# Forward attention of a fused block on Trainium2: the order of a step's score matmuls, P V and filler matmuls on TensorE

## The chip, the core and the metric

The kernel runs on one core of one Trainium2 chip. The metric is the device time in microseconds of one execution of the whole program. Each time of a kernel is a median of several executions; the profile is one further execution, recorded by the hardware profiler.

## What is computed

The program computes a transformer block with attention and a gated feed-forward part side by side, and the gradients of its six inputs, all in one launch. Cut to what matters:

```python
xn = layernorm(x)                                   # x: 1 x 2048 x 448
q, k, v = split(xn @ wqkv)                          # 16 heads of 28
p  = softmax(q @ k^T * 28**-0.5)                    # 16 x 2048 x 2048
o  = p @ v
y  = x + concat(o) @ wo + (silu(xn @ w_gate) * (xn @ w_up)) @ w_down   # F = 1792
out_0 = y;  out_1 .. out_6 = gradients for grad_out of x, wqkv, wo, w_gate, w_up, w_down
```

## The kernel before, in words

The instructions of every engine are issued in the order in which the Python code names them (`manual_schedule`, L59); each engine works its own list from front to back. Waits between engines are set by the tile framework, from the tiles that instructions read and write and from the buffers that a pool has to give.

The program has four stages: a prologue (layer norm, projections of head group 0), the forward loop (L588 to L621), the backward loop of attention (L830 to L915) with the remaining products of the feed-forward part between its matmuls, and a tail for the gradient of x.

The forward loop has 256 steps `(g, qc, kt)`: 4 groups of 4 heads, 4 chunks of 512 queries, 16 tiles of 128 keys. In one step:

- **Scores, two halves.** A head has 28 columns, padded to 32, so that the four heads of a group stand on the partitions 0, 32, 64 and 96 of `qT` and `kT`. One matmul (L600) with a contraction of 32 rows gives the transposed scores of one head, 128 keys x 512 queries. A *half* is two such matmuls, on two row tiles of TensorE: half 0 on rows 0 and 32, half 1 on rows 64 and 96. They fill one `s_ps` tile of two PSUM banks. The pool `ps_s` has two such buffers (L108), so half 0 of a step takes the buffer of half 0 of the step before, and half 1 that of half 1.
- **Exponentials.** Behind each half ScalarE runs one `Exp` over 128 x 1024 (L604) from `s_ps` into an `eT` tile in SBUF (seven buffers, L107).
- **P V.** `pv(i)` (L575 to L586) multiplies the four `eT` pieces of step i with the values of the four heads: four matmuls (L582) on four column tiles, summed over 16 steps in `o_ps`, a pool with one buffer (L109). In step i the call is `pv(i - 2)`, and it stands between the two halves (L606, L607). At the last key tile `pv` calls `o_items` (L467), which issues a ScalarE copy of `o_ps` (L470) and pushes four transposes and sixteen small matmuls, with their DMAs, to the front of the filler queue.
- **Fillers.** `fill(pace)` (L617) then takes other TensorE work from a queue: the three products of the feed-forward part (L383), its weight gradients (L357), the projections of the next head group (L180), the pushed items of `o_items`. Each has a fixed cost (`MM`, `MMD`), and `pace` (L594) is the cost that is left divided by the steps that are left. Fillers write to `ps_f` (three buffers). The last matmul of a gate product issues a `Tanh` on ScalarE (L393), and VectorE does the rest.

So TensorE's list for a step reads: half 0, P V of two steps ago, half 1, fillers. ScalarE's list reads: Exp 0, (copy of `o_ps` once in 16 steps), Exp 1, (Tanh once in some steps).

In the text, S0 and S1 are the two halves, E0 and E1 their exponentials, and F is the time from the first filler to the S0 of the next step.

Of the kernel before, what the change touches and what calls it, by code (L numbers as in the profile page):

```python
# [12 lines left out]
FP32 = mybir.dt.float32  # L13
# [11 lines left out]
P = 128  # L25
# [12 lines left out]
def kernel(  # L38
# [69 lines left out]
    ps_s = bst.enter_context(tc.tile_pool(name="ps_s", bufs=2, space=PSUM))  # L108
# [99 lines left out]
    def sp_layouts(g):  # L208
        for tq, dst in ((0, spq_d), (1, spk_d)):
            s_ = stg.tile([P, NT, P], BF16, name="sp_stage")  # L210
            sp.dma_start_transpose(out=s_[:], in_=qk_tiles[(g, tq)][:])
            pool.dma_start(out=dst[g], in_=s_[:].rearrange("p t c -> p (t c)"))
# [96 lines left out]
    def fill(budget):  # L309

        while budget > 0.05:
            if not cur:
                if not queue:
                    return
                cur.extend(queue.popleft())
            cost, fn = cur.popleft()
            fn()
            budget -= cost
            left[0] -= cost

    def push(jobs, front=False, behind=0):
        left[0] += sum(c for job in jobs for c, _ in job)
        if front:
            first = [queue.popleft() for _ in range(min(behind, len(queue)))]
            queue.extendleft(reversed(first + jobs))
        else:
            queue.extend(jobs)

    def proj_items(g):
        out = []  # L330
        for tq in range(3):
            for sc in range(4):
                box = {}

                def go(c, tq=tq, sc=sc, box=box):
                    if c == 0:
                        box["m"] = proj_unit(g, tq, sc, "dve")
                    box["m"](c)
                out.append([(MM, lambda c=c, go=go: go(c)) for c in range(4)])
        out.append([(0.0, lambda: proj_done(g))])  # L340
        return out
# [204 lines left out]
    def load_pair(pr, parts):  # L546

        g, r = pr // 2, 64 * (pr % 2)
        q = qkp.tile([P, S], BF16, name="qT")
        k = qkp.tile([P, S], BF16, name="kT")  # L550
        qd[pr] = (q, k)
        n = S // parts
        return [lambda i=i, dst=dst, r0=r0, src=src: sp.dma_start(
                    out=dst[r0:r0 + 64, i:i + n], in_=src[g, r:r + 64, i:i + n])
                for r0, srcs in ((0, (qT_d, kT_d)), (64, (dOT_d, vT_d)))
                for dst, src in zip((q, k), srcs) for i in range(0, S, n)]

    def load_group(g, parts, kpool):

        spt[g] = [qkp.tile([P, NT, P], BF16, name="v_sp"), kpool.tile([P, S], BF16, name="vT"),  # L560
                  qkp.tile([P, NT, P], BF16, name="O_sp")]
        spt[g][1] = spt[g][1][:].rearrange("p (t c) -> p t c", c=P)
        n = NT // parts
        return [lambda i=i, t=t, src=src: sp.dma_start(
                    out=t[:, i:i + n, :].rearrange("p t c -> p (t c)"), in_=src[g, :, i * P:(i + n) * P])
                for t, src in zip(spt[g], (spq_d, spk_d, spo_d)) for i in range(0, NT, n)]
# [6 lines left out]
    pv_next = [0]  # L573

    def pv(i):  # L575
        g, qc, kt = steps[i]
        if kt == 0:
            o_cur["o"] = ps_o.tile([P, 512], FP32, name="o_ps")
        o_ps, v = o_cur["o"], v_tiles[g]
        e = eTs.pop(i)  # L580
        for hh in range(4):
            pe.matmul(o_ps[HP * hh:HP * (hh + 1), :], lhsT=v[:, kt, HP * hh:HP * (hh + 1)],  # L582
                      rhs=e[hh // 2][:, hh % 2, :], start=(kt == 0), stop=(kt == NT - 1),
                      tile_position=(0, HP * hh), skip_group_check=True)
        if kt == NT - 1:
            o_items(g, qc, o_ps)  # L586

    for i, (g, qc, kt) in enumerate(steps):  # L588
        if kt == 0 and qc == 1:
            push([[(0.0, lambda g=g: sp_layouts(g))]], front=True)  # L590
        if kt == 0 and qc == 2 and g + 1 < G:
            push(proj_items(g + 1), front=True)
        qT, kT = qk_tiles[(g, 0)], qk_tiles[(g, 1)]
        pace = left[0] / (nst - i)  # L594
        eTs[i] = []
        for half in range(2):
            s_ps = ps_s.tile([P, 2, 512], FP32, name="s_ps")
            for j in range(2):
                r = HP * (2 * half + j)
                pe.matmul(s_ps[:, j, :], lhsT=kT[r:r + HP, kt * P:(kt + 1) * P],  # L600
                          rhs=qT[r:r + HP, qc * 512:(qc + 1) * 512],
                          start=True, stop=True, tile_position=(r, 0))
            e = ep.tile([P, 2, 512], BF16, name="eT")
            act.activation(out=e[:], in_=s_ps[:], func=ACT.Exp, scale=SCALE)  # L604
            eTs[i].append(e)
            if half == 0 and i >= 2:  # L606
                pv(i - 2)  # L607
        if g == G - 1 and qc == 2:
            if kt == 0:
                first = load_pair(0, 1) + load_group(0, 1, vp)  # L610
            elif kt % 2 and first:
                first.pop(0)()
        if i in (6, 8, 10, 12):
            j = i // 2 - 3
            sp.dma_start_transpose(out=woT[:, :, j * P:(j + 1) * P], in_=wo_pad[:, j, :])
        pv_next[0] = max(0, i - 1)
        fill(pace)  # L617
    while pv_next[0] < nst:
        pv(pv_next[0])
# [210 lines left out]
    for k in range(N + 2 * UW):  # L830
        W, pos = k // UW, k % UW
        if k < N:
# [16 lines left out]
            s_ps = ps_sd.tile([P, 2, 512], FP32, name="sd")  # L849
# [162 lines left out]
```

## Time and profile before

| | |
|---|---|
| median of 3 runs | 1563.34 us (1561.85 to 1567.34) |
| the profiled execution | 1562.89 us, of which the profile's span is 1561.1 us |
| forward loop in the trace | S0 of the first step at 31.1 us, S1 of the last at 664.4 us |
| TensorE matmuls (PE) busy | 1447.1 us of the span |
| ScalarE (ACT) busy | 1190.1 us |
| VectorE (DVE) busy | 1098.9 us |

How to read it: PE stands for TensorE's matmuls and PEld for its weight loads. Matmuls are pipelined, so that two that follow each other overlap in the records; the distance from one start to the next is what a matmul costs its engine, not its recorded duration. A row of the timeline has the start, the time until the last of its instructions ended, the engine, the line, what is written from what, the shapes, and how many instructions it joins; in brackets stand the idle time of the engine ahead of it and what ended it. A row of a stretch has its length and, for each engine, busy time and number of instructions, then the granted TensorE clock, the share of the DMA engines in use and GB/s.

### The profile page before, as it was taken

The numbers are of one execution on the slowest core, as the hardware profiler recorded it, in microseconds if no ns is written. First come the engines' busy times: TensorE is split into PE (matmuls) and PEld (weight loads), VectorE is DVE, ScalarE is ACT, GpSimd is POOL, SyncE is SP. The second block draws the span as 40 slices with busy tenths as digits, with TensorE's granted clock in tenths as the row PEclk, the third lists the DMA queues.
The fourth block names the chain that finished last, engine by engine and source line by source line (L and its number), as shares of the span: only waits on it lengthen the run. The fifth ranks groups of instructions, "written<-read, shape, count | busy, mean of one in ns | idle before, by whom it ended". The sixth has DMA issues, their size and how long they took to land.

```text
span 1561.1 us, 32024 instructions
## 1 busy us (share of the span) xinstructions
PE 1447.1 (93%) x12176; PEld 606.3 (39%) x12176; DVE 1098.9 (70%) x1421; ACT 1190.1 (76%) x1333; POOL 396.1 (25%) x664
## 2 busy tenths in 40 slices
PE   6999999899999999988998988989999899999986
PEld 3233333333333333333333444434335333544353
DVE  7664655455655666467877887979888789888925
ACT  6899998688787877766776777878778778888823
POOL 4342333344434444411010111110102111111033
PEclk9999999899999999989999999999999999999998
DMA  9985756875967699879999999999999999999993
GB/s 231 190 162 120 145 116 137 164 146 127 198 131 155 134 186 212 170 164 222 204 214 200 192 202 217 198 197 200 207 208 199 196 194 196 185 188 213 184 281 123
DMA packets 682106, 285.12 MB, mean 183 GB/s; under 512 B 637136, under 2 KB 650464, under 8 KB 681952
## 3 DMA queue, kind: packets, MB, share of 16 engines
q1 hardware_dynamic: 652016, 210.03, 72.7%
q0 software_dynamic: 25968, 64.53, 17.1%
q10 hardware_dynamic: 3968, 8.52, 1.6%
q8 instruction: 95, 1.56, 0.4%
q14 instruction: 59, 0.48, 0.1%
HBM read 67.34 MB, written 63.44 MB: 84 GB/s over the span
## 4 chain that ended last, share of the span: by engine, by line
PE 63%; DMA 14%; ACT 9%; DVE 6%; issue 5%; SPq 1%; POOL 1%; DVEq 0%; POOLq 0%; ACTq 0%
PE s_ps L600 8%; PE f_ps L357 8%; DMA dsT<-ds 8%; PE f_ps L383 7%; PE sd L851 6%; ACT E L869 5%; PE acc L748 4%; PE aux L718 4%; PE o_ps L582 4%; PE aux L775 4%; PE aux L795 4%; DVE ds L880 3%; PE aux L712 3%; ACT dsT L782 3%; PE sd L862 3%
## 5 line engine op out<-in xcount | busy, mean ns | idle before, releaser
L880 DVE TENSOR_TENSOR ds<-sd,E 128x1024 bf16<-128x1024 f32 x512 | 611.2, 1220 | 131.8 <-DMA dsT<-ds 47.8
L869 ACT ACTIVATE E<-sd 128x1024 bf16<-128x1024 f32 x512 | 516.7, 1024 | 171.7 <-PE sd L862 133.6
L604 ACT ACTIVATE eT<-s_ps 128x1024 bf16<-128x1024 f32 x512 | 497.9, 1024 | 103.8 <-PE s_ps L600 102.9
L862 PE MATMUL sd<-kT,qT 32*128 32x512 bf16 x1024 | 203.2, 390 | 23.6 <-ACT E L869 22.7
L851 PE MATMUL sd<-kT,qT 32*128 32x512 bf16 x1024 | 201.9, 391 | 20.1 <-DVE ds L880 17.9
L748 PE MATMUL acc<-ds,v_sp 128*32 128x512 bf16 x1024 | 205.7, 397 | 0.7 <-DVE ds L880 0.7
L748 PE MATMUL acc<-E,O_sp 128*32 128x512 bf16 x1024 | 205.5, 397 | 0.2 <-ACT dkv_o L754 0.2
L600 PE MATMUL s_ps<-qT,kT 32*128 32x512 bf16 x1024 | 200.1, 388 | 1.5 <-ACT eT L604 1.1
L422 POOL DMA_DIRECT2D hd_d<-fT x168 | 126.8, 767 | 17.2 <-DVE fT L407 9.9
L383 PE MATMUL f_ps<-xnT,wgu 128*128 128x512 bf16 x448 | 120.2, 387 | 3.4 <-DVE w_sb L409 3.4
L763 POOL DMA_DIRECT2D dqkv_d<-dkv_o x64 | 39.3, 619 | 293.1 <-ACT dkv_o L754 290.9
L600 PEld LDWEIGHTS <-kT 32*128 32x128 bf16 x1024 | 48.7, 91 | 159.8 <-issue 158.1
L718 PE MATMUL aux<-W,ck 128*128 128x448 bf16 x448 | 107.1, 356 | 3.3
L851 PEld LDWEIGHTS <-qT 32*128 32x128 bf16 x1024 | 51.0, 91 | 149.2 <-issue 141.2
L582 PE MATMUL o_ps<-eT,v_sp 128*32 128x512 bf16 x1024 | 103.2, 394 | 0.0
L357 PE MATMUL f_ps<-xn_sp,f_sp 128*128 128x448 bf16 x448 | 99.1, 354 | 0.0
L748 PEld LDWEIGHTS <-O_sp 128*32 128x32 bf16 x1024 | 50.4, 93 | 113.5 <-issue 103.7
L775 PE MATMUL aux<-ident_bf,ds 128*128 128x128 bf16 x1024 | 81.6, 224 | 11.6 <-DVE dq_acc L807 5.7
L862 PEld LDWEIGHTS <-qT 32*128 32x128 bf16 x1024 | 65.0, 91 | 61.7 <-issue 57.8
L357 PEld LDWEIGHTS <-f_sp 128*128 128x128 bf16 x672 | 58.3, 98 | 73.8 <-issue 23.7
L775 PEld LDWEIGHTS <-ds 128*128 128x128 bf16 x1024 | 63.7, 100 | 40.9 <-issue 40.2
L395 DVE SCALAR_TENSOR_TENSOR g<-t_sb,f_ps 128x512 f32<-128x512 f32 x56 | 38.5, 687 | 55.4 <-ACT t_sb L393 55.3
(133 smaller groups left out, 1759.8 us busy)
## 6 DMA issues: line engine op xcount, KB each, us to landing
hd_d<-fT POOLq DMA_DIRECT2D x168, 128.0 KB, 4.6
ck<-hd_d SPq DMA_DIRECT2D x32, 448.0 KB, 4.4
ck<-hd_d SPq DMA_DIRECT2D x16, 576.0 KB, 4.9
dsT<-ds SPq DMA_TRANSPOSE x384, 4.1
dqkv_d<-dkv_o POOLq DMA_DIRECT2D x64, 64.0 KB, 3.7
dq_c<-dqkv_d ACTq DMA_DIRECT2D x5, 768.0 KB, 6.8
W<-wT_d SPq DMA_DIRECT2D x14, 224.0 KB, 3.6
out_dram<-dw_o POOLq DMA_DIRECT2D x28, 96.0 KB, 4.0
```

The lines of the kernel that those rows point to most:

```text
L357: pe.matmul(acc[:, :D], lhsT=src[:, 12 * (t // 4) + 4 * wi + t % 4, :], rhs=rhs[:, t, :D], start=(t == 0), stop=(t == NT - 1))
L383: pe.matmul(st[name][:], lhsT=w(c), rhs=src[:, tsl, c, :], start=(c == 0), stop=(c == 3))
L582: pe.matmul(o_ps[HP * hh:HP * (hh + 1), :], lhsT=v[:, kt, HP * hh:HP * (hh + 1)], rhs=e[hh // 2][:, hh % 2, :], start=(kt == 0), stop=(kt ...
L600: pe.matmul(s_ps[:, j, :], lhsT=kT[r:r + HP, kt * P:(kt + 1) * P], rhs=qT[r:r + HP, qc * 512:(qc + 1) * 512], start=True, stop=True, tile_ ...
L604: act.activation(out=e[:], in_=s_ps[:], func=ACT.Exp, scale=SCALE)
L718: return [lambda n=n: pe.matmul(ps[:, :D], lhsT=t[:, n, :], rhs=w[:, n, :], start=(n == 0), stop=(n == NFC - 1)) for n in range(NFC)]
L748: pe.matmul(acc[r:r + HP, :], lhsT=src[:, qt, 64 * hp + HP * j:64 * hp + HP * j + HP], rhs=m[:, j, :], start=(qt == 0), stop=(qt == NT - 1 ...
L775: pe.transpose(ps[:, i, :], ds[:, i // 4, (i % 4) * P:(i % 4 + 1) * P], ident_bf[:])
L851: pe.matmul(s_ps[:, j, :], lhsT=q[HP * j:HP * j + HP, qt * P:(qt + 1) * P], rhs=kv[HP * j:HP * j + HP, kc * 512:(kc + 1) * 512], start=Tru ...
L862: pe.matmul(d_ps[:, j, :], lhsT=q[r:r + HP, qt * P:(qt + 1) * P], rhs=kv[r:r + HP, kc * 512:(kc + 1) * 512], start=True, stop=True, tile_p ...
L869: act.activation(out=E[k][:], in_=s_ps[:], func=ACT.Exp, scale=SCALE)
L880: dve.tensor_tensor(out=DS[k - 1][:], in0=d_ps[:], in1=E[k - 1][:], op=ALU.mult)
```

## The change

Both `s_ps` tiles of a step are taken first, and the four score matmuls are issued directly behind each other, on the row tiles 0, 32, 64 and 96. Then come both exponentials in ScalarE's list. P V of the step just passed, `pv(i - 1)` in place of `pv(i - 2)`, is issued behind all four score matmuls, and the fillers follow. After the loop one P V is left in place of two.

```diff
         eTs[i] = []
-        for half in range(2):
-            s_ps = ps_s.tile([P, 2, 512], FP32, name="s_ps")
+        pair = [ps_s.tile([P, 2, 512], FP32, name="s_ps") for _ in range(2)]
+        for half, s_ps in enumerate(pair):
             for j in range(2):
                 r = HP * (2 * half + j)
                 pe.matmul(s_ps[:, j, :], lhsT=kT[r:r + HP, kt * P:(kt + 1) * P],
                           rhs=qT[r:r + HP, qc * 512:(qc + 1) * 512],
                           start=True, stop=True, tile_position=(r, 0))
+        for s_ps in pair:
             e = ep.tile([P, 2, 512], BF16, name="eT")
             act.activation(out=e[:], in_=s_ps[:], func=ACT.Exp, scale=SCALE)
             eTs[i].append(e)
-            if half == 0 and i >= 2:
-                pv(i - 2)
+        if i >= 1:
+            pv(i - 1)
...
-        pv_next[0] = max(0, i - 1)
+        pv_next[0] = i
         fill(pace)
```

## The prediction

> **What bounds the kernel now.** I read the page first (engine totals, the costliest groups), then the stretches of the forward loop, then its timeline step by step.
>
> ```profile
> PE 1447.1 (93%) x12176; PEld 606.3 (39%) x12176; DVE 1098.9 (70%) x1421; ACT 1190.1 (76%) x1333; POOL 396.1 (25%) x664
> ...
> L604 ACT ACTIVATE eT<-s_ps 128x1024 bf16<-128x1024 f32 x512 | 497.9, 1024 | 103.8 <-PE s_ps L600 102.9
> ```
>
> TensorE is busy 93% of the span, and ScalarE's exponentials of the forward loop wait 102.9 us for scores: there TensorE sets the pace. The change touches this loop alone, so I cut it into five stretches, first all engines, then the exponentials alone (their count, halved, is the number of steps).
>
> ```profile
> 37.00:120.00 83.00, 79.36 (x491) 27.27 (x488) 51.84 (x90) 72.91 (x82) 32.50 (x46) 0.96 0.94 182
> 120.00:240.00 120.00, 119.69 (x775) 43.65 (x775) 63.99 (x111) 108.78 (x121) 36.76 (x55) 1.00 0.63 127
> 240.00:400.00 160.00, 154.79 (x957) 55.98 (x955) 88.06 (x152) 130.95 (x145) 61.60 (x91) 0.96 0.73 148
> 400.00:520.00 120.00, 117.71 (x744) 44.30 (x743) 71.39 (x124) 96.76 (x107) 48.79 (x72) 1.00 0.77 154
> 520.00:664.00 144.00, 140.50 (x873) 52.88 (x871) 83.94 (x144) 111.72 (x124) 64.90 (x93) 1.00 0.87 179
> ```
> ```profile
> 37.00:120.00 83.00, 68.55 (x71) 0.96 0.94 182
> 120.00:240.00 120.00, 104.09 (x109) 1.00 0.63 127
> 240.00:400.00 160.00, 123.67 (x128) 0.96 0.73 148
> 400.00:520.00 120.00, 90.77 (x94) 1.00 0.77 154
> 520.00:664.00 144.00, 103.80 (x107) 1.00 0.87 179
> ```
>
> The first number behind the length is PE's busy time: 96 to 100% of each stretch, while ACT (the fourth) falls from 91% of its stretch in the second row to 78% in the last. PE busy per step, call it L, is 79.36 / 35.5 = 2.235 us, then 119.69 / 54.5 = 2.196, 154.79 / 64 = 2.419, 117.71 / 47 = 2.504, 140.50 / 53.5 = 2.626. I use L and not the bare length, so that TensorE's stalls stay out of it; the change doesn't remove those.
>
> One step, from the timeline:
>
> ```profile
> 402.23 0.39 PE L600 MATMUL s_ps<-qT,kT 32*128 32x512 bf16 x2
> ...
> 402.55 0.40 PE L582 MATMUL o_ps<-eT,v_sp 128*32 128x512 bf16 x4
> ...
> 402.72 1.94 ACT L604 ACTIVATE eT<-s_ps 128x1024 bf16<-128x1024 f32 x2 [0.46 <-PE s_ps L600]
> ...
> 402.88 0.39 PE L600 MATMUL s_ps<-qT,kT 32*128 32x512 bf16 x2
> ...
> 403.20 0.74 PE L357 MATMUL f_ps<-xn_sp,f_sp 128*128 128x448 bf16 x3
> ...
> 404.73 0.39 PE L600 MATMUL s_ps<-qT,kT 32*128 32x512 bf16 x2
> ```
>
> S0 takes 0.32 us to the next start, P V 0.33, S1 0.32, the fillers F = 1.53: a step is 0.97 + F. E0 starts 0.49 after S0, and the two exponentials end 1.94 later, 2.43 after S0. S1 needs the buffer that E1 of the step before has read. Here it starts 0.65 behind S0, and TensorE hardly ever waits for that:
>
> ```profile
> PE s_ps L600 <- ACT eT L604: 0.6, 3, 0.2
> ```
>
> **The change part by part.** *Four row tiles beside each other.* The forward trace has the quad once, in step 0, and the backward loop has it in every step:
>
> ```profile
> 852.79 0.39 PE L851 MATMUL sd<-kT,qT 32*128 32x512 bf16 x2
> ...
> 852.80 0.39 PE L862 MATMUL sd<-kT,qT 32*128 32x512 bf16 x2
> ...
> 853.12 1.12 PE L712 MATMUL aux<-W,ck 128*128 128x448 bf16 x5
> ```
>
> Two pairs on rows 0, 32 and 64, 96 start 0.01 apart, and the next work starts 0.33 after the first: a quad costs what a pair costs. So TensorE's own work falls by one pair of 0.32 a step, to 0.66 + F: 254.5 steps x 0.32 = 81 us in all five stretches, if nothing waits.
>
> *The wait that comes in.* S1 now stands directly behind S0, and its buffer is free only when E1 of the step before has ended. P V used to fill this time; now P V and the fillers stand in TensorE's list behind the waiting S1. What that looks like is in the trace, since the first two steps have no P V:
>
> ```profile
> 31.14 0.39 PE L600 MATMUL s_ps<-qT,kT 32*128 32x512 bf16 x4
> ...
> 31.47 1.25 PE L383 MATMUL f_ps<-xnT,wgu 128*128 128x512 bf16 x5
> 31.57 1.94 ACT L604 ACTIVATE eT<-s_ps 128x1024 bf16<-128x1024 f32 x2 [1.47 <-PE s_ps L600]
> ...
> 32.65 0.10 PEld L600 LDWEIGHTS <-kT 32*128 32x128 bf16 x3 [0.42 <-issue]
> 32.66 0.39 PE L600 MATMUL s_ps<-qT,kT 32*128 32x512 bf16 x2
> ...
> 33.56 0.39 PE L600 MATMUL s_ps<-qT,kT 32*128 32x512 bf16 x2 [0.52 <-ACT eT L604]
> 33.56 0.09 PEld L600 LDWEIGHTS <-kT 32*128 32x128 bf16 x1 [0.82 <-issue]
> ...
> 33.89 0.82 PE L383 MATMUL f_ps<-xnT,wgu 128*128 128x512 bf16 x3
> ...
> 35.07 0.39 PE L600 MATMUL s_ps<-qT,kT 32*128 32x512 bf16 x2
> ```
>
> Step 0 is a quad. Its exponentials end at 31.57 + 1.94 = 33.51; S0 of step 1 is out at 32.66, S1 waits until 33.56, the fillers stand behind it, and S0 of step 2 comes at 35.07. So a loop closes over two steps: S0, Exp 0 and Exp 1, S1 of the next step, its P V, its fillers, S0 of the step after. Its length is 0.49 (S0 to Exp 0; 0.43 in these rows) + 1.94 + 0.05 (33.51 to 33.56) + 0.32 + 0.33 + F = 3.13 + F for two steps. With 0.43 and without P V it gives 0.43 + 1.94 + 0.05 + 0.32 + 1.19 = 3.93, the 35.07 - 31.14 of the rows.
>
> A step after is therefore the larger of 0.66 + F and (3.13 + F) / 2 = 1.565 + F / 2; the second holds until F = 1.81. Typically a step without a wait is followed by one in which S1 waits 1.81 - F. Before, the same loop was shorter by P V's 0.33, 1.40 + F / 2 a step, and below 0.97 + F for every F above 0.86: not binding.
>
> The gain of a step is 0.97 + F - 1.565 - F / 2, or, with F = L - 0.97, L / 2 - 1.08:
>
> - first stretch: 0.038 x 35.5 = 1.3 us
> - second: 0.018 x 54.5 = 1.0
> - third: 0.130 x 64 = 8.3
> - fourth: 0.172 x 47 = 8.1
> - fifth: 0.233 x 53.5 = 12.5
>
> Together 31.2 us of the possible 81. The late steps pay because they have more fillers.
>
> *ScalarE's other work, whose cover shrinks.*
>
> ```profile
> L393 ACT ACTIVATE t_sb<-f_ps 128x512 f32<-128x512 f32 x56 | 33.8, 603 | 3.8 <-PE f_ps L383 3.2 <-ACT eT L604 0.3
> L470 ACT COPY o_raw<-o_ps 128x512 f32<-128x512 f32 x16 | 9.3, 581 | 0.8 <-PE o_ps L582 0.8
> ...
> 77.28 3.81 ACT L604 ACTIVATE eT<-s_ps 128x1024 bf16<-128x1024 f32 x4
> ```
>
> Four exponentials in a row take 3.81, so one adds (3.81 - 1.02) / 3 = 0.93, a pair 1.86, and a Tanh or copy about 0.48 beyond the overlap of 0.1. Before, the idle time ahead of Exp 0 (0.46 in the step shown) hid them. After, two steps leave 3.13 + F - 3.72 = 0.6 to 1.0 us, nearly all in the long one. I take it that half of the 72 fall in the short step, stick out by 0.3 on average (0.48 at F = 1.2, 0.1 at 1.6), and that half of that comes back, since the next S1 then waits less: 72 x 0.5 x 0.3 x 0.5 = 5.4. Bounds: 0, and all exposed, 72 x 0.48 = 34.6.
>
> *P V one step earlier.* Its exponentials are done, since S1 waited for them. What it issues moves with it: the copy of `o_ps`, the queued transposes, small matmuls and their DMAs on SP's and POOL's queues, the same number in the same order, one step earlier among 256; nothing. But the copy now stands behind both exponentials, and the next P V needs the one `o_ps` buffer: the copy ends 0.48 after Exp 1, so that P V starts at 0.53 where it would start at 0.05 + 0.32 = 0.37: 16 x 0.16 = 2.6 at most. I take 1.4.
>
> *DMA and clock.* Same transfers in a loop 4% shorter; the DMA share of the last stretch is 0.87. I take nothing for contention, with the price among the rivals.
>
> ```profile
> 1200.00:1400.00 200.00, 184.72 (x2043) 85.80 (x2035) 173.31 (x165) 158.24 (x171) 31.54 (x76) 1.00 1.07 195
> ```
>
> The granted clock is 1.00 in three of the five stretches. TensorE's gaps of up to 0.6 us are new there; in this stretch of the backward loop it idles 15 us of 200 with the clock at 1.00. So nothing for the clock either.
>
> Sum: 31.2 - 5.4 - 1.4 = 24.4 us. Against the profiled execution's 1562.9 (its span of 1561.1 and 1.8 around it) that gives **1538.5 us**; the median of the runs, 1563.3, is 0.4 higher, which I don't add.
>
> **The rivals.**
>
> *Both buffers are taken at once* (slower). The change asks for both `s_ps` tiles ahead of the first matmul. If that makes S0 wait for Exp 1 too, no scores are made during an exponential, and a step is the larger of 0.66 + F and 0.49 + 1.94 + 0.05 = 2.48. Against L: +0.245 x 35.5 = 8.7, +0.284 x 54.5 = 15.5, +0.061 x 64 = 3.9, -0.024 x 47 = -1.1, -0.146 x 53.5 = -7.8, sum +19: 1582 us. It decides where F is below 1.51. For it: the order of the code. Against: waits here stand at matmuls, not at allocations (three weight loads ran at 32.65, one of them for S1, whose matmul waited until 33.56), and each buffer has its own reader.
>
> *No wait at all*: TensorE alone sets the pace and the whole 81 us come: 1481. By throughput it could: PE 612 - 81 = 531 over the stretches, ScalarE 254.5 x 1.86 + 72 x 0.48 = 508. Against: S1 needs 2.48 from the S0 before, and 0.66 + F is less nearly everywhere. The Trainium skill, in TensorEngine Tiling, section PSUM Bottleneck, warns that tiling speeds TensorE up but not the emptying of PSUM, which may become the bottleneck. Taken as throughput, 508 below 531, the rule leaves the 81 us whole; the rows of step 1 say that the handover of two buffers binds before.
>
> *Half comes back through DMA*: a transposed `f_sp` or weight lands no earlier, and TensorE waits there instead.
>
> ```profile
> 290.95 1.67 PE L357 MATMUL f_ps<-dy_sp,f_sp 128*128 128x448 bf16 x4 [4.51 <-DMA f_sp<-fT]
> ```
>
> One such wait is there, 4.51 us, in the third stretch. Three more of them, in the last two stretches, cost 13: 1552. For it the share of 0.87; against, that the other filler waits of the loop are few.
>
> *ScalarE's small work all exposed*: 31.2 - 34.6 - 1.4, 4.8 us lost: 1568, at the edge of no change by the bound below. Against: in the long step there is room.
>
> **How the numbers follow.** Forecast 0.64; half back through DMA 0.16; no wait at all 0.03; small work exposed 0.05; both buffers at once 0.12. The forecast alone runs from 1524 (small work free: -6.8; 0.43 for 0.49: -0.06 x 127 = -7.6) to about 1546 (0.06 the other way); the DMA case to 1556. These hold 0.80, so the range is 1522 to 1558, and the two slower cases and the largest gain stay out. A measurement of this kernel tells about 0.3% from no change, that is 4.7 us: faster 0.83, the same 0.04, slower 0.13.
>
> **What would show it.** In the changed profile: L600 in fours with the next start 0.33 later where S1 doesn't wait; S1 alone, 0.2 to 0.6 after S0, "<-ACT eT", in about every second step, with TensorE's total of that wait near 81 - 31 = 50 us in place of 0.6; step lengths that alternate; the first 200 us of the loop hardly shorter, the last 150 shorter by 0.2 a step; the backward loop as long as before. If S0 too waits for ScalarE in most steps, the first rival is right; if the wait for `f_sp` grows, the third. The forecast is wrong if the quad takes 0.6, or if Exp 0 starts later than 0.5 after S0.

## The result and the profile after

The changed kernel takes 1547.84 us (median of 5 runs, 1541.70 to 1549.43) against 1561.85 us of the kernel before in runs beside it (5 runs): ratio 0.991, 95% interval 0.9882 to 0.9937, some 14 us faster. The forecast was 1538.5 us, 24.4 us faster, in a range of 1522 to 1558: the right side and the right mechanism, with a gain that came out 10 us smaller.

The page of the changed kernel, the lines that answer to those quoted above, with the line of the score matmuls:

```profile
span 1547.7 us, 32024 instructions
...
PE 1412.8 (91%) x12176; PEld 597.7 (39%) x12176; DVE 1099.4 (71%) x1421; ACT 1187.9 (77%) x1333; POOL 396.1 (26%) x664
...
L605 ACT ACTIVATE eT<-s_ps 128x1024 bf16<-128x1024 f32 x512 | 495.8, 1026 | 93.1 <-PE s_ps L600 89.6
...
L600 PE MATMUL s_ps<-qT,kT 32*128 32x512 bf16 x1024 | 148.0, 386 | 7.8 <-ACT eT L605 5.6
```

The line of the score matmuls in the kernel before:

```profile
L600 PE MATMUL s_ps<-qT,kT 32*128 32x512 bf16 x1024 | 200.1, 388 | 1.5 <-ACT eT L604 1.1
```

TensorE is busy 34 us less and the span is 13.4 us shorter; of the score matmuls' busy time, 200.1 us before, 52 us have gone.

Where the span changed is read from the first and last start of two lines, the score matmuls of the forward loop (L600) and those of the backward loop (L851 before, L852 after). Kernel before, then the changed one; behind the median duration stand first and last start:

```profile
L600 PE MATMUL s_ps<-qT,kT x1024: 371/385/605, 31.1 to 664.4; 32*128 32x512 bf16 x171
...
L851 PE MATMUL sd<-kT,qT x1024: 371/385/605, 672.9 to 1480.3; 32*128 32x512 bf16 x171
```
```profile
L600 PE MATMUL s_ps<-qT,kT x1024: 371/384/604, 30.7 to 647.8; 32*128 32x512 bf16 x171
...
L852 PE MATMUL sd<-kT,qT x1024: 371/385/604, 656.4 to 1470.0; 32*128 32x512 bf16 x171
```

I call the time between the two first starts the forward stage, and that between the first and the last start of the second line the backward stage. Forward: 672.9 - 31.1 = 641.8 us before, 656.4 - 30.7 = 625.7 after, 16.1 less. Backward: 807.4 and 813.6, with untouched code; a second trace of the changed kernel shows 817.3, and the other traces of this study lie between 807 and 815. So the backward stage scatters by some us from execution to execution, and a single pair of traces can't charge those 6 us to the change. The forward stage is what carries the result. It too is read from one trace of each kernel, and differences of a few us between two traces should not be leaned on.

Two neighbouring steps of the changed kernel, from its timeline (PE and ACT rows):

```profile
113.28 0.39 PE L600 MATMUL s_ps<-qT,kT 32*128 32x512 bf16 x4
...
113.60 0.40 PE L582 MATMUL o_ps<-eT,v_sp 128*32 128x512 bf16 x4
...
113.77 3.78 ACT L605 ACTIVATE eT<-s_ps 128x1024 bf16<-128x1024 f32 x4 [0.55 <-PE s_ps L600]
...
113.94 1.25 PE L180 MATMUL f_ps<-xnT,W 128*128 128x512 bf16 x5
...
115.12 0.39 PE L600 MATMUL s_ps<-qT,kT 32*128 32x512 bf16 x2
115.76 0.39 PE L600 MATMUL s_ps<-qT,kT 32*128 32x512 bf16 x2 [0.25 <-ACT eT L605]
...
116.08 0.40 PE L582 MATMUL o_ps<-eT,v_sp 128*32 128x512 bf16 x4
...
117.60 0.40 PE L600 MATMUL s_ps<-qT,kT 32*128 32x512 bf16 x4
```

The first step is a quad: four score matmuls, P V 0.32 us later, the next S0 after 1.84 us. In the second, S0 is out at 115.12, S1 waits for the exponential until 115.76, and P V stands behind it; this step takes 2.48. The four exponentials of the two steps run in one piece, and ScalarE has idled 0.55 us ahead of them. The two steps take 4.32 us, where the kernel before takes 2 x 2.16 at this place (S0 at 117.92 and again at 120.08): nothing gained. Steps don't alternate so strictly everywhere: by the starts in the trace, S1 follows within 0.05 us of S0 in 83 of the 256 steps and comes later in the other 173, by 54 us in all. Late in the loop, with more fillers:

```profile
597.36 0.40 PE L600 MATMUL s_ps<-qT,kT 32*128 32x512 bf16 x4
...
598.02 1.69 PE L357 MATMUL f_ps<-xn_sp,f_sp 128*128 128x448 bf16 x8
...
599.64 0.59 PE L600 MATMUL s_ps<-qT,kT 32*128 32x512 bf16 x4
```

This step takes 2.28 us, where before a step with such fillers takes 2.59 (S0 at 597.80 and at 600.39). The joined row at 599.64 lasts 0.59 and not 0.39: there S1 started some 0.2 us after S0, and the row shows this wait as busy time.

TensorE's waits over the forward stage of the changed kernel (total, times, longest):

```profile
PE f_ps L479 <- ACT o_raw L470: 8.8, 8, 1.8
PE f_ps L357 <- DMA f_sp<-fT: 8.1, 2, 7.0
PE s_ps L600 <- ACT eT L605: 5.6, 19, 0.5
```

Before, the second of these was 4.5 us, and the first 1.8:

```profile
PE f_ps L479 <- ACT o_raw L470: 1.8, 3, 0.7
```

That the first has grown is new, and the forecast didn't have it:

```profile
106.12 1.94 ACT L605 ACTIVATE eT<-s_ps 128x1024 bf16<-128x1024 f32 x2
...
107.93 0.60 ACT L470 COPY o_raw<-o_ps 128x512 f32<-128x512 f32 x1
108.58 0.20 PEld L479 LDWEIGHTS f_ps<-ident_f,o_raw 128*128 128x128 f32 x2 [1.72 <-ACT o_raw L470]
108.58 0.44 PE L479 MATMUL f_ps<-ident_f,o_raw 128*128 128x128 f32 x2 [1.22 <-ACT o_raw L470]
```

At the last key tile the copy of `o_ps` stands in ScalarE's list behind both exponentials of the step. The transposes that read the copy are pushed to the front of the filler queue, so TensorE reaches them in the same step, waits 1.22 us, and everything behind them waits too.

### The profile page after: what moved, and what is told of

The parts are those of the page before. It is cut to its first block, busy times and chain, and to the rows that moved or that the text cites. A ratio compares the mean times of both kernels' runs of the same rounds, so it can differ in the third digit from the quotient of the medians.

```text
span 1547.7 us, 32024 instructions
## 1 busy us (share of the span) xinstructions
PE 1412.8 (91%) x12176; PEld 597.7 (39%) x12176; DVE 1099.4 (71%) x1421; ACT 1187.9 (77%) x1333; POOL 396.1 (26%) x664
## 4 chain that ended last, share of the span: by engine, by line
PE 56%; DMA 13%; ACT 13%; DVE 8%; issue 6%; SPq 1%; POOL 1%; ACTq 0%; DVEq 0%; POOLq 0%
DMA dsT<-ds 9%; PE f_ps L357 7%; PE sd L852 6%; PE s_ps L600 6%; PE f_ps L383 6%; ACT E L870 5%; PE aux L719 4%; PE acc L749 4%; PE aux L796 4%; PE aux L776 4%; PE o_ps L582 4%; ACT eT L605 4%; DVE ds L881 3%; ACT dsT L783 3%; PE aux L713 3%
## 5 line engine op out<-in xcount | busy, mean ns | idle before, releaser
L605 ACT ACTIVATE eT<-s_ps 128x1024 bf16<-128x1024 f32 x512 | 495.8, 1026 | 93.1 <-PE s_ps L600 89.6
L852 PE MATMUL sd<-kT,qT 32*128 32x512 bf16 x1024 | 201.8, 390 | 24.7 <-DVE ds L881 22.3
L600 PE MATMUL s_ps<-qT,kT 32*128 32x512 bf16 x1024 | 148.0, 386 | 7.8 <-ACT eT L605 5.6
L383 PE MATMUL f_ps<-xnT,wgu 128*128 128x512 bf16 x448 | 118.8, 383 | 4.9 <-DVE w_sb L409 4.7
L852 PEld LDWEIGHTS <-qT 32*128 32x128 bf16 x1024 | 51.3, 91 | 154.1 <-issue 145.5
L582 PE MATMUL o_ps<-eT,v_sp 128*32 128x512 bf16 x1024 | 103.4, 394 | 0.6
L600 PEld LDWEIGHTS <-kT 32*128 32x128 bf16 x1024 | 40.7, 91 | 137.7 <-issue 132.7
```

Source lines behind the costliest of these rows:

```text
L383: pe.matmul(st[name][:], lhsT=w(c), rhs=src[:, tsl, c, :], start=(c == 0), stop=(c == 3))
L852: pe.matmul(s_ps[:, j, :], lhsT=q[HP * j:HP * j + HP, qt * P:(qt + 1) * P], rhs=kv[HP * j:HP * j + HP, kc * 512:(kc + 1) * 512], start=Tru ...
```

## The experiments

The theory after the result: (a) the loop over the two `s_ps` buffers holds the step, as forecast; (b) the row tiles' concurrency is what brings the gain; (c) what is missing went into the transposes' wait for the copy. The rival to (c) is that the gain came back through DMA, at the `f_sp` wait. The first four kernels bear on (c), the next four on (a) and (b), the last four on what these left open. The forward stage of each is read as above, from one trace.

**The changed kernel again.**

> The changed kernel itself, beside the three others on the same chip: 1548 within 4 us, with another trace of the forward and the backward loop. Theory: forward loop (first score matmul to first score matmul of the backward loop) 626 us within 4, as in the first trace; the backward loop, whose code is untouched, scatters by some us from execution to execution, so that the 6 us by which it was longer in the first trace of the changed kernel are not an effect of the change. Rival (the change makes the backward loop longer): again 813 us against 807.

1552.58 us; before, in the runs beside it, 1564.69; ratio 0.9928 (0.9894 to 0.9962). Forward stage 626.1 us, backward stage 817.3. The time is 0.6 us outside the 4 expected, beside a kernel before that was 2.8 us longer too, and the forward stage came out as expected. The backward stage was again long, as the rival said. Two kernels in the old order of the forward loop, further down, show 811.5 and 812.4, which speaks for scatter, but no run settles it.

**The copy between the exponentials.**

```diff
-        for s_ps in pair:
+        for half, s_ps in enumerate(pair):
             e = ep.tile([P, 2, 512], BF16, name="eT")
             act.activation(out=e[:], in_=s_ps[:], func=ACT.Exp, scale=SCALE)
             eTs[i].append(e)
-        if i >= 1:
-            pv(i - 1)
+            if half == 0 and i >= 1:
+                pv(i - 1)
```

> The changed kernel with one edit: in ScalarE's list P V's copy of o_ps stands between the two exponentials of a step, as before the change, and not behind both. TensorE's list is unchanged. Theory (the handover loop holds, and the 8 us that the forward loop lacks against the forecast are the transposes of o_items, which wait for the copy behind both exponentials): TensorE's wait of the transposes (L479) for the copy falls from 8.8 us to under 3, and the time falls by 4 to 8 us against the changed kernel's 1548, to 1540 to 1544; not the whole 8, because the copy now delays the second exponential. Rival (the 8 us came back through DMA waits): the L479 wait falls all the same, but waits for f_sp grow and the time stays at 1548.

1549.62 us, ratio 0.9906 (0.9872 to 0.994); forward stage 624.7. The transposes wait 3.4 us in place of 8.8, a little above the 3 expected, but the time is within the interval of the unchanged version, where 4 to 8 us were expected. The copy now stands ahead of the second exponential, on which the next S1 waits (L600 busy 150.9 us in place of 148.0, and 6.4 in place of 5.6 us of idle time); waits of fillers for VectorE grew as well (L180 behind L409: 4.6 us in place of 2.2). By these figures the wait was moved more than removed.

**The copy on VectorE.**

```diff
-        act.copy(out=o_raw[:], in_=o_ps[:])
+        dve.tensor_copy(out=o_raw[:], in_=o_ps[:])
```

> The changed kernel with the copy of o_ps on VectorE in place of ScalarE. Theory: the copy no longer waits for exponentials and takes nothing from ScalarE: the L479 wait falls under 3 us and the time by 6 to 9 us, to 1539 to 1542, unless VectorE's own list holds the copy up. Rival (DMA): 1548.

1552.68 us, ratio 0.9921 (0.9896 to 0.9946); forward stage 628.4: a miss, since the wait was to fall under 3 us and the time by 6 to 9. TensorE's waits over the forward stage of this kernel:

```profile
PE f_ps L357 <- DMA f_sp<-fT: 9.1, 2, 8.3
PE f_ps L479 <- DVE o_raw L470: 8.9, 6, 2.6
...
PE o_ps L582 <- DVE o_raw L470: 4.0, 4, 1.6
```

The transposes wait as long as in the changed kernel, now for a copy that stands in VectorE's list, and P V waits 4.0 us more for the one `o_ps` buffer.

**The transposes later.**

```diff
-             + (dwo_items(g) if qc == 3 else []), front=True, behind=1)
+             + (dwo_items(g) if qc == 3 else []), front=True, behind=3)
```

> The changed kernel with the items of o_items queued behind three filler groups in place of one, so that the transposes are issued one to three steps later. The copy stays where the change put it. Theory: the copy is long done when the transposes come, the L479 wait goes, and the time falls by 5 to 8 us, to 1540 to 1543. Rival (DMA): 1548; or later, if what hangs on the transposes becomes late.

1536.73 us, ratio 0.9815 (0.9775 to 0.9854), 16 us below the changed kernel beside it and twice the 8 us that were expected at most; forward stage 607.9. Its waits:

```profile
PE s_ps L600 <- ACT eT L605: 5.5, 22, 0.5
...
PE f_ps L357 <- DMA f_sp<-fT: 1.0, 1, 1.0
...
PE f_ps L479 <- ACT o_raw L470: 0.7, 1, 0.7
```

The copy is early enough without being moved: the wait of the transposes is down to 0.7 us. But the long wait for `f_sp` has gone too, which the theory had not asked for. In the trace of the changed kernel that wait costs more than its 7 us:

```profile
546.35 1.30 PE L357 MATMUL f_ps<-dy_sp,f_sp 128*128 128x448 bf16 x3 [7.05 <-DMA f_sp<-fT]
...
547.58 0.61 PE L600 MATMUL s_ps<-qT,kT 32*128 32x512 bf16 x4
```

The matmuls behind it last 0.61 in place of 0.39 us: TensorE ran slower for a while after the stall. The granted clock was 0.50 from 546.3 to 550 us, 0.86 in the next 2 us, and 1.00 again from 552. In the kernel before it was 0.50 from 290.9, the end of the wait of 4.51 us, to 300, and 0.63 to 304.

**Half of the exponentials.**

```diff
-            act.activation(out=e[:], in_=s_ps[:], func=ACT.Exp, scale=SCALE)
+            act.activation(out=e[:, 0, :], in_=s_ps[:, 0, :], func=ACT.Exp, scale=SCALE)
...
-                      rhs=e[hh // 2][:, hh % 2, :], start=(kt == 0), stop=(kt == NT - 1),
+                      rhs=e[hh // 2][:, 0, :], start=(kt == 0), stop=(kt == NT - 1),
```

> The changed kernel with half the exponentials left out: each reads one of the two banks of its s_ps tile, and P V uses that half for both heads; matmuls, DMAs and order are unchanged. Theory (the loop over the handover of the two buffers holds the step): with exponentials of some 0.55 us the loop is 0.49 + 1.1 + 0.05 + 0.65 + F for two steps, below 2 x (0.66 + F), so S1 never waits, L600 is busy some 100 us in place of 148, and the rest of the 81 us comes, 50 to 58 us less than the changed kernel: 1490 to 1498 (up to 1505 if DMA waits take some). Rival (TensorE's own work or DMA holds the step): less than 20 us, above 1528.

1507.36 us, before beside it 1559.03, ratio 0.9659 (0.9617 to 0.9702); forward stage 581.0. From its page and its timeline:

```profile
L605 ACT ACTIVATE eT<-s_ps 128x512 bf16<-128x512 f32 x512 | 277.8, 595 | 248.6 <-PE s_ps L600 248.6
...
L600 PE MATMUL s_ps<-qT,kT 32*128 32x512 bf16 x1024 | 102.4, 390 | 0.0
```
```profile
113.80 0.40 PE L600 MATMUL s_ps<-qT,kT 32*128 32x512 bf16 x4
...
115.64 0.40 PE L600 MATMUL s_ps<-qT,kT 32*128 32x512 bf16 x4
```

With shorter exponentials S1 never waits, every step is a quad, and a step takes 1.84 us where the changed kernel alternated 1.84 and 2.48 at this place. The rival is out: some 40 us more came (0.9659 against 0.991 to 0.9928), not under 20. It is less than the 50 expected, and 1507 lies above the 1505 allowed for. Other waits grew in the faster loop: 15.9 us for VectorE at L180 and L383, where the changed kernel has 6.9, and 3.9 for `dyT`; the wait for `f_sp` stayed, with 7.8.

**The same half in the kernel before.**

> The kernel before with the same half of the exponentials left out. Theory: TensorE alone sets the pace of the forward loop there, so ScalarE's shorter work is worth nothing but small waits: 1556 to 1562. Rival (exponentials slow TensorE down otherwise, by PSUM or clock): 20 us or more below the kernel before.

1553.33 us, ratio 0.9965 (0.9939 to 0.9991): 5.7 us less, and 2.7 below the low end. Its forward stage is 625.1 us, 16.7 less than in the one trace of the kernel before; but the long wait for `f_sp`, with the slow clock behind it, is absent here (1.3 us in place of 4.5). Against the kernel further down that keeps all exponentials and lacks this wait as well (627.1), it is 2.0 us. So in the old order shorter exponentials are worth little, in the new order some 40 us.

**The shorter lag alone.**

```diff
-            if half == 0 and i >= 2:
-                pv(i - 2)
+            if half == 0 and i >= 1:
+                pv(i - 1)
...
-        pv_next[0] = max(0, i - 1)
+        pv_next[0] = i
```

> One part of the change alone: the kernel before, with P V of the step just passed, pv(i - 1) in place of pv(i - 2), still between the halves. P V now waits for the second exponential of the step before, and S1 stands behind it. Theory: the same loop, 3.13 + F for two steps, but a step of 0.97 + F where nothing waits, so no gain anywhere: 0 to 6 us slower than before, 1562 to 1568. Rival (the shorter lag itself brings the gain): 1548 to 1555.

1572.17 us, ratio 1.0085 (1.0053 to 1.0116), 13 us slower, beyond the 6 expected. Its steps are those of before:

```profile
121.72 0.39 PE L600 MATMUL s_ps<-qT,kT 32*128 32x512 bf16 x2
122.04 0.40 PE L582 MATMUL o_ps<-eT,v_sp 128*32 128x512 bf16 x4
122.37 0.39 PE L600 MATMUL s_ps<-qT,kT 32*128 32x512 bf16 x2
122.69 1.25 PE L180 MATMUL f_ps<-xnT,W 128*128 128x512 bf16 x5
123.88 0.39 PE L600 MATMUL s_ps<-qT,kT 32*128 32x512 bf16 x2
```

2.16 us for a step with five fillers, P V between the halves, no wait. What is longer are the waits for `f_sp`: 7.8 us, two in place of one, and the one for VectorE at L180, 4.0 in place of 1.5. The forward stage is 650.7 us. So the lag gains nothing by itself; that the 13 us came through `f_sp`, by moving `o_items` a step, fits these waits but was not tried apart.

**The order without the four row tiles.**

```diff
-                r = HP * (2 * half + j)
+                r = HP * j
```

> The changed kernel with S1 on the same two row tiles as S0 (heads 0 and 1 are computed twice, heads 2 and 3 left out): the order of the change without the four row tiles beside each other. Theory (the gain is the concurrency of the row tiles): S0 and S1 now take 0.22 + 0.32 in place of 0.33, a step is 0.87 + F or the loop; late steps gain 0.1, early ones nothing, and the wait for the copy stays: 1552 to 1562. Rival (the gain comes from the order alone, one change of tiling less a step): 1548 as the changed kernel.

1559.53 us, ratio 0.999 (0.9965 to 1.0016); forward stage 633.3; L600 busy 166.0 us. Inside the range expected, and no gain against before that is clear of noise. Its forward stage is 8.5 us shorter than in the one trace of before, so the order alone may bring a little, as was expected of late steps. The rest of the gain is the concurrency of the row tiles.

**The transposes later in the kernel before** (the edit of `behind` above).

> The kernel before, with the items of o_items queued behind three filler groups, as in the version of the changed kernel that came out 16 us shorter. Theory (the later place removes the waits of the transposes and, by alignment, the one long wait for f_sp, in either kernel; what the change of order brings beside that is the forecast's 24 us): before gains the 10 us of its long wait with the slow clock behind it and some 2 of the transposes, 1549 to 1556, and the changed kernel with the same later place (1537) stays 12 to 20 us, forward loop 20 to 26 us, ahead of it. Rival (the later place helps only the new order): 1562, and the gap is 25 us or more.

1552.13 us, before beside it 1559.02, ratio 0.9951 (0.9929 to 0.9972); forward stage 627.1. The old order too loses its long wait for `f_sp`:

```profile
PE f_ps L383 <- DVE w_sb L409: 5.1, 5, 1.3
PE f_ps L180 <- DVE w_sb L409: 2.6, 1, 2.6
...
PE f_ps L479 <- ACT o_raw L470: 0.7, 1, 0.7
PE s_ps L600 <- ACT eT L604: 0.5, 1, 0.5
```

So with both waits out of both kernels the change is worth 627.1 - 607.9 = 19.2 us of the forward stage, just under the 20 to 26 expected, and by the ratios 0.9815 / 0.9951 = 0.986, some 21 us.

**The old lag in the new order.**

```diff
-        if i >= 1:
-            pv(i - 1)
+        if i >= 2:
+            pv(i - 2)
...
-        pv_next[0] = i
+        pv_next[0] = max(0, i - 1)
```

> The changed kernel with the old lag: P V of two steps ago behind the four score matmuls. Theory: P V never waited in the changed kernel, so the lag is worth nothing in the loop; o_items comes one step later, in the same place of a step, and its transposes wait as long for the copy (L479, 7 to 9 us). Time as the changed kernel, within 6 us, unless the long wait for f_sp falls away by alignment (then 8 less). Rival (the shorter lag costs, as in the run with the lag alone, which was 13 us slower): 8 to 13 us less than the changed kernel, with all its other steps shorter too.

1543.24 us, ratio 0.9904 (0.9878 to 0.9931), as the changed kernel; forward stage 627.1. The transposes wait 7.5 us, as expected. The wait for `f_sp` fell to 1.6, but the 8 us that were to go with it did not: fillers wait 7.8 us for VectorE at L383 in place of 4.7, and 4.4 in place of 2.2 at L180. P V hardly waits in the changed kernel (0.6 us of idle time ahead of L582), and its lag shows no worth here.

**The store of `oT` on POOL.**

```diff
-            sp.dma_start(out=hd_d[tsl, :, g, :].rearrange("k p s -> p k s"),
+            pool.dma_start(out=hd_d[tsl, :, g, :].rearrange("k p s -> p k s"),
```

> The changed kernel, with the store of oT to hd_d (L494) issued by POOL and not by SP. On SP it waits for the transposition of oT to land, 16 times 2.7 us, with all that SP issues behind it. Theory (the long wait for f_sp comes from SP's list: the f_sp transposition stands behind this store): f_sp lands earlier, TensorE's wait for it (7 to 8 us) falls to under 4, and the time falls by 3 to 8 us, the waits for the copy staying. Rival (the transposition itself is slow, from contention among DMAs): the wait stays and the time too.

1551.45 us, ratio 0.9942 (0.9919 to 0.9965); forward stage 628.0, and the wait for `f_sp` 7.5 us, as long as in the changed kernel. The theory that moving this store frees TensorE falls. The trace shows where it went: the transposition of `f_sp` is issued 7.9 us after `fT` is written, where the changed kernel needs 10.7, but takes 7.9 us to land in place of 4.6.

**Both: the transposes later, the store on POOL.**

> Both edits together: the changed kernel with the items behind three groups and the store of oT on POOL. Theory: the first already removed both waits, so the store adds little: as the version with the later place, 0.98 to 0.985 of before. Rival (SP's list is late elsewhere too): 4 us or more below it.

1535.21 us, ratio 0.9846 (0.9815 to 0.9877); forward stage 609.0. The store adds nothing. Of the kernels that leave nothing out, the two in the new order with the later transposes are the fastest of this study, both clear of the changed kernel. This one ran beside the kernel before with later transposes (1552.13), and is 16.9 us below it: the worth of the change with both waits out, once more.

## Why the prediction was right, and where it was not

**What bounds the loop**: right. TensorE set the pace before: leaving out half of the exponentials was worth 5.7 us there.

**A quad costs what a pair costs**: right. 0.32 us from the quad to P V in the changed kernel; and with S1 kept on S0's rows the gain went (0.999).

**The wait that comes in**: right to the hundredth in the two steps shown. The loop of 3.13 + F gives 4.32 us for two steps at F = 1.19, and 1.84 + 2.48 were measured. Early steps gained nothing; the last 31 gained some 0.2 on average (84.5 us before, 77.3 after), 0.3 where nothing waits. Over the whole last stretch of the prediction's table it is only 0.05 a step, since the wait of 7 us for `f_sp` stands in it, and 0.14 with the transposes later in both kernels. Taking ScalarE's time away freed most of the rest. Of the Trainium skill's warning in TensorEngine Tiling (Array Packing), section PSUM Bottleneck, the runs show the part that holds here: the emptying of PSUM does become the limit, but by the handover of two buffers, with ScalarE still idle 93.1 us ahead of its exponentials.

**TensorE's wait "near 50 us"**: the size was right, the view wrong. The row of waits shows 5.6 us. The rest hides in L600's busy time, since S1 waits while S0 still counts as busy: 148.0 us, against 102.4 where S1 never waits, is 45.6, with the 5.6 together 51; the starts of S1 behind S0, 54 us in all, say the same. The sign expected was S1 alone in about every second step; it was so in two of three. The Trainium skill, in Trainium Kernel Development and Optimization, section Performance Expectations, calls matmul busy time a bad metric for how close a kernel is to roofline, the limit of the hardware, because matmuls are pipelined. That is another use of the number; here it hid nine tenths of a wait.

**P V one step earlier**: this is the step that failed. The prediction counted P V's own wait for the `o_ps` buffer, 1.4 us of at most 2.6, and called the order of the queued transposes unchanged. The first was fair: in 7 of the 16 groups the first P V starts 0.16 us later, 1.1 us. The order is unchanged too; but the copy moved from between the exponentials to behind both, and the transposes, first in the filler queue, wait for it: 8.8 us in place of 1.8, so 7.0 us. That this place causes the wait is shown by the copy between the exponentials (3.4 us left) and by the later transposes (0.7). That the copy's place can be mended with profit is not shown: between the exponentials it cost elsewhere what it saved.

**Half comes back through DMA**: it happened in part. The `f_sp` wait is 8.1 us (6.7 in the second trace) where it was 4.5, and the clock stays low for some us behind it. 24.4 - 7.0 - 3.6 = 13.8 us is what the forecast gives with both waits put in, close to the 14.0 of the medians. That closeness is luck in part. Putting the transposes later took both waits out, and it was worth 641.8 - 627.1 = 14.7 us of the forward stage in the old order and 625.7 - 607.9 = 17.8 in the new: by these traces the two waits explain 3.1 us of what is missing, by the medians (6.9 and 15.9 us) 9, and not 10.6. So theory (c) holds for the wait, and for the time only in part.

**L, the step's busy time**: a term that was too large. With both waits absent from both kernels the change brings 19.2 us in the forward stage, 5 less than forecast. By the prediction's stretches, cut at the same steps, the two kernels with later transposes differ by 0.1, 0.9, 3.8, 6.9 and 7.2 us, where the sum had 1.3, 1.0, 8.3, 8.1 and 12.5 ahead of the small terms of 6.8. The prediction's own rows show a granted clock of 0.96 in the first and the third stretch; in the kernel before with later transposes it is 1.00 in both. So L held slow time, by estimate 0.04 x 83 + 0.04 x 160 = 9.7 us, and a gain of L / 2 - 1.08 counts half of it, 4.9 us, as gained. That is about what these two stretches lack. What is missing in the fifth is of the size of the small terms (Tanh and copies beside the exponentials); no run separates them.

**Both buffers taken at once, no wait at all, small work all exposed**: none of the three. S0 runs while the second exponential of the step before is still on (115.12 in the rows above).

**Why `f_sp` comes late**: the traces show it, though no run tried it alone. In the changed kernel the transposition that TensorE waits for isn't slow. It is issued late:

```profile
530.33 0.68 DVE L417 SCALAR_TENSOR_TENSOR fT<-f_ps,w_sb 128x512 bf16<-128x512 f32 x1
```
```profile
533.56 3.11 SPq L211 DMA_TRANSPOSE sp_stage<-kT  x1
536.77 1.22 SPq L492 DMA_TRANSPOSE oT<-O_sp  x1
539.31 0.36 SPq L494 DMA_DIRECT2D hd_d<-oT  x1
539.77 1.82 SPq L523 DMA_TRANSPOSE dOT<-dOl  x1
541.67 1.57 SPq L419 DMA_TRANSPOSE f_sp<-fT  x1
```

Its input is written at 531.0, it is issued at 541.7, and it lands 4.6 us later; the median of the 56 of this trace is 4.8. Ahead of it in SP's list stand the transposition of `kT`, which waits until POOL's store has emptied the one `sp_stage` buffer, and the three DMAs of `o_items`. With the transposes later these three come behind `f_sp`, and TensorE reaches the reader of `f_sp` 12.3 us after `fT` is written in place of 8.3, while it lands after 13.3 in place of 15.3: the wait is 1.0 us. In the kernel before the cause was another: issued 1.9 us after `fT`, the transposition landed 14.3 us later, behind that of `v_sp` ahead of it, which landed at 287.4.

**Still open**: what a change of SP's list would bring, why the transposition takes 7.9 us with the store on POOL, and what separates the small terms.

## What to carry to other kernels

Two buffers between two engines make a loop over two steps: the producer's start, both consumer passes, the second producer, and all that stands behind it until the next start. Work moved from ahead of the waiting instruction to behind it lengthens that loop; add it up before counting the matmul time saved. And where a step is moved, follow what it issues on other engines to its first reader: a copy one place later in ScalarE's list brought 7.0 us of waiting where 1.4 had been counted, and putting the reader later was a better cure than moving the copy, in part for a reason nobody had planned, the DMAs that moved with it. And busy time that was measured under a slow clock is not all work that a change can save.

## What was not expected of the hardware

A wait can stand inside a busy row: two matmul pairs 0.2 us apart are shown as one row of 0.59 us with no idle time. After a stall of 7 us TensorE's next matmuls took 0.61 in place of 0.39 us, at a granted clock of 0.50 for some 4 us, so that a long wait costs more than its length. A wait for a DMA need not mean a slow DMA: this one landed in the usual 4.6 us and had stood 10.7 us in its queue's list. And a stage with untouched code, the backward loop, lasted 807 to 817 us from trace to trace, where the effect that was measured is 14.
